# A state-space convolution and a gated MLP on one core: each queue's order written down instead of list scheduled

## The chip, the cores and the metric

The kernel runs on one core of one Trainium2 chip, in one launch. The metric is the device time in microseconds (us) from one execution; a kernel's time is the median of its runs. The core has five engines with a queue of instructions each: TensorE (PE, matmuls), VectorE (DVE), ScalarE (ACT), GpSimd (POOL) and SyncE (SP, which here only issues DMAs). ACT and POOL issue some DMAs too.

## What is computed

The reference adds three terms for x of 2048 positions and 640 channels. With `xn` the layer norm of x over the channels:

```
out = x + S4(xn) + gMLP(xn)
S4:   K[d,l] = Re( sum_n C[d,n] * exp(dt[d]*A[d,n]*l) * dt[d]*B[d,n] )     128 complex states per channel
      y = causal convolution of xn with K along the 2048 positions (by FFT of length 4096) + xn*Dskip
gMLP: z = gelu(xn @ w_in), w_in 640 x 1728;  z1, z2 = halves of z, 864 columns each
      g = w_sp @ layernorm(z2) + b_sp, w_sp 2048 x 2048
      (z1*g) @ w_out, w_out 864 x 640
```

Inputs and output are bf16.

## The kernel before, in words

**Stages.** The gMLP is made of large matmuls on the whole 128x128 array: mm1b and mm1a (xn by the two halves of w_in, 16 blocks each of 2x5 matmuls of 432 columns, followed by a gelu on ACT), ln2 (layer norm of z2 on DVE, its last step "flexible", see below), mm2 (16 blocks x 2 halves x 16 matmuls of 432 columns with w_sp, whose transposed tiles come by DMA, then one `gate` operation on DVE and a store of the gated rows to DRAM, `zg_scratch`), and mm3 (by w_out, with the gated rows read back by transposing DMAs, `zgt`).

The S4 part first generates the kernel K in two halves of ten chunks (class Kgen, `chunks` at L1234): for each chunk `trig` (sines, with small matmuls "kpe" on 32-row tiles of the array, 32x384, 32x128 and 32x272), `mags` (exponentials), `products` ("kprod", L1204, DVE), and `contract` ("kcon", L1218): 64 matmuls of 128x33 on four tiles of 32 columns, then the evacuation "kevac". The convolution is a two-stage transform (class Conv): `expand` (L1308) sends a half of K through DRAM (`k2d_scratch`) and into a layout for the transform, sixteen DMAs by SP and eight by ACT's queue, `stage1` ("st1", 128x256 on the whole array, evacuation "ev1"), `stage2` ("st2", L1352, 64x160 on two tiles of 64 rows, evacuations "ev2u" for the input and "ev2k" for the kernel, then the product "pw" on DVE), a swap of halves by DMA ("uswap"), `inverse1` ("inv1", 128x128, evacuation "evz") and the last transform "inv2" (32x160 on sixteen tiles of 32x32). inv2 and mm3 add into the same PSUM banks, and the output leaves from there.

A tile of the array is a rectangle of it with weights of its own, named by `tile_position`. In kcon and stage 2 the innermost loop runs over the tiles:

```
L1225  for jl in range(NJ):                      # 8
           for m in range(2):
               for g in range(4):
                   B.mm(pt[32*g : 32*g+NT, ...], ..., start=(m == 0), stop=(m == 1), tile_position=(0, 32*g))
L1359  for k in range(nf):
           for c in range(2):
               for jj in range(2):
                   h = 64*jj
                   B.mm(..., start=(c == 0), stop=(c == 1), tile_position=(h, 0))
```

**What sets the order.** A Builder first records every operation in program order, with what it reads and writes (5325 operations, 4282 on PE). `schedule()` (L384) then picks an order for each of the five queues, and `emit()` (L528) derives the semaphores and writes the instructions[...]. Some evacuations, copies and scalings are flexible (`flex`, L299, `flexn`, L308): they may run on ACT or on DVE, in the two engines' own instruction.

`schedule()` is a list scheduler. It keeps modelled times of each queue and each operation, and at each step picks a ready operation by priority: the longest path to the end, plus a bonus, plus an amount per kind of operation (`local`, L1734), plus an amount per group of operations (`SHIFT`, L771, 661 numbers). A change of the array's shape costs 0.095 us in its model (0.2 us when leaving 32-column tiles), a change of ACT's table 1.4 us. Flexible operations go to whichever engine is picked first, with `flexpen` (L1733) against DVE for two kinds.

The lines of the profile that follow: L341 is every matmul (`mm`), L348 PE transposes, L263 every ACT activation, L273 and L285 DVE tensor operations (L285 the gate), L293 and L304 copies, the latter flexible ones on DVE, L375 DMAs, L382 transposing DMAs. So groups are told apart by operand shape.

Of the kernel before, what the change touches and what calls it, by code (L numbers as in the profile page):

```python
# [65 lines left out]
class Builder:  # L66
# [317 lines left out]
    def schedule(self):  # L384
        ops = self.ops
        n = len(ops)
        succ = [[] for _ in range(n)]
        npred = [0] * n
        for op in ops:
            seen = set()  # L390
            for d in op.deps + op.odeps:
                if d.gidx in seen:
                    continue
                seen.add(d.gidx)
                succ[d.gidx].append(op)
                npred[op.gidx] += 1
        group = -1
        last = None
        shift = []
        for op in ops:  # L400
            if op.tag != last:
                group += 1
                last = op.tag
            shift.append(SHIFT[group] if SHIFT else 0)
        plen = [0.0] * n
        for op in reversed(ops):
            best = 0.0
            bmax = op.bonus
            for s_ in succ[op.gidx]:
                if plen[s_.gidx] > best:  # L410
                    best = plen[s_.gidx]
                if s_.bonus > bmax:
                    bmax = s_.bonus
            plen[op.gidx] = best + op.dur + (op.lat if op.is_dma else 0.0)
            op.bonus = bmax
            op.prio = plen[op.gidx] + bmax + self.local.get(op.tag, 0.0) + shift[op.gidx]
        ready = {q: [] for q in QUEUES}

        def make_ready(op):
            for q in (("act", "dve") if op.alt else (op.q,)):  # L420
                ready[q].append(op)

        for op in ops:
            op.t0 = None
            if npred[op.gidx] == 0:
                make_ready(op)
        tfree = {q: 0.7 for q in QUEUES}
        flight = {q: [] for q in QUEUES}
        CAP = 120
        cur_tab = None  # L430
        cur_mode = None
        dma_free = 0.0
        TABSW = 1.4
        MODESW = {(128, 32): 0.2}
        WIN = 2.0
        WINP = 0.1
        order = []
        petimes = []
        nsched = 0
        while nsched < n:  # L440
            bestq = None
            for q in QUEUES:
                cand = ready[q]
                if not cand:
                    continue
                evals = []
                base = tfree[q]
                if q == "pe" and len(petimes) >= 128:
                    base = max(base, petimes[-128] + 3.2)
                for op in cand:  # L450
                    ts = base + (MODESW.get(cur_mode, 0.095) if q == "pe" and op.mode != cur_mode else 0.0)
                    for d in op.deps:
                        t = d.t1 + (0.057 if q == "pe" else 0.035)
                        if t > ts:
                            ts = t
                    for d in op.odeps:
                        if d.t0 > ts:
                            ts = d.t0
                    if q == "dve" and op.alt:
                        ts += self.flexpen.get(op.tag, 0.0)  # L460
                    rt = ts
                    if q == "act" and op.tab is not None and op.tab != cur_tab:
                        ts += TABSW
                    evals.append((ts, op, rt))
                tmin = min(e[0] for e in evals)
                pick = None
                for ts, op, rt in evals:
                    if ts <= tmin + (WINP if q == "pe" else WIN):
                        if pick is None or op.prio > pick[1].prio:
                            pick = (ts, op, rt)  # L470
                gap = None
                for ts, op, rt in evals:
                    back = MODESW.get(op.mode, 0.095) if q == "pe" and op.mode != pick[1].mode else 0.0
                    if ts + op.dur + back <= pick[2 if q in ("act", "pe") else 0] + 0.02 and (gap is None or op.prio > gap[1].prio):
                        gap = (ts, op, rt)
                if gap is not None:
                    pick = gap
                if bestq is None or pick[0] < bestq[0]:
                    bestq = (pick[0], pick[1], q)
            ts, op, q = bestq  # L480
            if op.alt:
                op.q = q
                op.emit, op.dur = op.alt[q]
                if q == "dve":
                    ts -= self.flexpen.get(op.tag, 0.0)
            if q == "act" and not op.is_dma and cur_tab is None and op.tab is None:
                ts += 1.3
                cur_tab = "none"
            op.t0 = ts
            if op.is_dma:  # L490
                start = max(ts + op.dur + 0.7, dma_free)
                dma_free = start + op.lat
                op.t1 = max(dma_free, ts + op.dur + 1.0) + 1.0 + op.late
            else:
                op.t1 = ts + op.dur + (op.lat if q == "pe" else 0.083)
            tfree[q] = ts + op.dur
            if op.is_dma:
                fl = flight[q]
                fl.append((dma_free - op.lat, dma_free, op.npk))
                left = 0  # L500
                for a, b, k in reversed(fl):
                    if left + k > CAP:
                        tfree[q] = max(tfree[q], b - (CAP - left) / k * (b - a))
                        break
                    left += k
            if q == "act" and op.tab is not None:
                cur_tab = op.tab
            if q == "pe":
                cur_mode = op.mode
                petimes.append(op.t0)  # L510
            for q2 in (("act", "dve") if op.alt else (q,)):
                ready[q2].remove(op)
            order.append(op)
            nsched += 1
            for s_ in succ[op.gidx]:
                npred[s_.gidx] -= 1
                if npred[s_.gidx] == 0:
                    make_ready(s_)
        order.sort(key=lambda o: (o.t0, o.gidx))
        self.ops = order  # L520
        self.qops = {q: [] for q in QUEUES}
        for i, op in enumerate(order):
            op.gidx = i
            op.idx = len(self.qops[op.q])
            self.qops[op.q].append(op)
        self.est_time = max(o.t1 for o in order)
# [189 lines left out]
class Psum:  # L716
# [54 lines left out]
SHIFT = [  # L771
    292.2, 1391.7, 2926.2, 561.5, 4282.2, 0.0, 2464.1, 366.2, -1.3, 2095.2, 394.9, -6.4, 721.6, 288.5, 0.0, 561.5, 201.7, 7.0,
    615.9, -45.8, -1168.9, 949.4, -194.4, -36.5, -1185.4, -303.8, -215.4, 59.3, 0.0, 0.0, 2191.5, 632.2, 688.9, 1082.1, -171.1,
    -193.0, -30.1, 199.4, -1314.7, -1347.1, -3793.2, -1646.2, -27.5, -2166.0, -310.6, -2172.9, -1840.9, -5938.5, -1378.4,
    -1199.0, 680.3, 175.2, -29.4, 7463.7, 1298.2, 98.9, 91.3, 1676.7, 846.7, 1227.3, 236.0, 1866.9, -339.0, 3716.3, 147.3,
    854.7, 390.5, 2928.5, 21.9, 1945.2, 579.7, 7007.6, -488.7, -1849.5, 4059.8, 0.7, 423.9, 31.0, 2.6, -0.2, 3991.7, -466.5,
    3680.8, -1812.8, 2137.0, -1632.9, 222.4, 0.5, -1194.4, -761.7, -3318.7, -2388.7, -1746.3, -101.5, 364.7, 676.6, -60.0,
    608.1, -2172.5, -60.0, -96.1, 445.2, 2190.8, 1135.2, 583.4, 80.5, 1311.8, -117.4, -290.7, -33.9, 703.7, 415.2, 67.6, -766.3,
    -129.8, -7054.1, 229.2, -3288.8, -898.9, -330.0, -341.9, -1257.9, 105.6, -2259.6, -1176.8, 3406.7, -594.9, 843.2, -139.9,
    957.2, 2718.9, -374.2, -35.1, -885.8, 1787.8, -183.1, 3595.1, 2420.5, -292.2, -1089.0, -395.3, -1298.2, -280.3, -28.1, 21.7,  # L780
    -791.4, 0.0, 1963.3, 946.1, 1151.7, 2527.5, -408.6, -146.3, 0.0, 816.6, -66.0, 0.2, 2123.5, 0.0, -4548.3, -299.3, 772.2,
    0.0, 24.8, 25.3, -1418.1, -681.6, -1782.0, -1405.0, -49.2, -1346.2, 111.2, -649.5, 1185.3, -797.1, -524.2, -4443.6, -770.4,
    -1733.8, -2177.1, -1539.6, -435.2, -543.3, 0.0, -1346.0, 440.6, -2121.5, -700.2, 716.5, 0.0, 496.3, 772.4, -124.3, 970.3,
# [35 lines left out]
EXP_ = 2500.0  # L819
# [966 lines left out]
```

## Time and profile before

| what | value |
|---|---|
| runs of the kernel | 338.49, 340.62 and 589.61 us, median 340.62 |
| span of the profiled execution, first to last instruction | 337.6 us |
| PE busy | 314.9 us (93%), 4282 matmuls |
| PE loading weights | 210.1 us (62%) |
| DVE busy | 264.4 us (78%), 501 instructions |
| ACT busy | 230.4 us (68%), 267 instructions, 17 table loads of 1.283 us among them |
| DMA | 48.67 MB, mean 144 GB/s; 82153 of 102356 packets under 512 B |
| changes of the array's shape between matmuls in program order | 172 |
| operations that set PE's bound: 128x432 matmuls | 172.3 us for 832 |

The profiled execution's own device time is not listed apart from its span; the median of the runs is 3.0 us above this span. A row of the profile's groups names a line, an engine, an operation and the operand shapes, then count, busy time and the mean time in flight of one; several matmuls are in flight at once, so the mean is not what one costs. The end of a matmul is modelled in the trace, its start is recorded, so matmuls are best compared by the distance of their starts. "Idle before" is how long an engine stood still ahead of a group, with what released it. In the row of slices, each digit is the busy share of 1/40 of the span in tenths, and PEclk is the granted clock of PE in tenths of full speed.

### The profile page before, as it was taken

The numbers are of one execution on the slowest core, as the hardware profiler recorded it, in microseconds if no ns is written. First come the engines' busy times: TensorE is split into PE (matmuls) and PEld (weight loads), VectorE is DVE, ScalarE is ACT, GpSimd is POOL, SyncE is SP. The second block draws the span as 40 slices with busy tenths as digits, with TensorE's granted clock in tenths as the row PEclk, the third lists the DMA queues.
The fourth block names the chain that finished last, engine by engine and source line by source line (L and its number), as shares of the span: only waits on it lengthen the run. The fifth ranks groups of instructions, "written<-read, shape, count | busy, mean of one in ns | idle before, by whom it ended". The sixth has DMA issues, their size and how long they took to land.

```text
span 337.6 us, 9918 instructions
## 1 busy us (share of the span) xinstructions
PE 314.9 (93%) x4282; PEld 210.1 (62%) x4282; DVE 264.4 (78%) x501; ACT 230.4 (68%) x267; POOL 17.7 (5%) x34
## 2 busy tenths in 40 slices
PE   3999999989999999999999999997999989999972
PEld 2445467756556665556656586764689776679751
DVE  5998999998898997579999875968773676872373
ACT  3598989998665559684489976615688866337531
POOL 4211000212100000000000000000002000000001
PEclk9999999999999999999999999998999999999995
DMA  7994648544992555698899959799456999200056
GB/s 216 362 377 170 95 103 229 118 121 112 163 145 61 106 95 113 137 231 139 67 143 154 244 100 224 163 211 113 73 109 143 131 180 198 98 2 2 2 143 174
DMA packets 102356, 48.67 MB, mean 144 GB/s; under 512 B 82153, under 2 KB 100170, under 8 KB 101802
## 3 DMA queue, kind: packets, MB, share of 16 engines
q1 hardware_dynamic: 97256, 44.74, 65.6%
q0 software_dynamic: 448, 2.79, 4.7%
q10 hardware_dynamic: 4610, 0.53, 2.0%
q8 instruction: 33, 0.54, 0.7%
q14 instruction: 9, 0.07, 0.1%
HBM read 18.47 MB, written 11.61 MB: 89 GB/s over the span
## 4 chain that ended last, share of the span: by engine, by line
PE 71%; ACT 9%; DVE 7%; DMA 5%; issue 2%; ACTq 2%; SPq 2%; POOL 1%; POOLq 0%; DVEq 0%
PE ps L341 71%; ACT arena L263 6%; DVE arena L1516 3%; ACT L263 3%; DMA arena<-in_A_u_dram 3%; ACTq L375 2%; DVE arena L273 2%; SPq L382 1%; DMA arena<-xn_scratch 1%; DMA xn_scratch<-arena 1%; DVE arena L280 1%; SPq L375 1%; POOL arena L271 0%; DVE arena L285 0%; DVE arena L313 0%
## 5 line engine op out<-in xcount | busy, mean ns | idle before, releaser
L341 PE MATMUL ps<-arena 128*24 128x33 bf16 (+10 forms) x4222 | 311.8, 268 | 14.7 <-ACT arena L263 5.5
L341 PEld LDWEIGHTS ps<-arena 128*128 128x128 bf16 (+5 forms) x4222 | 206.2, 115 | 116.4 <-ACT arena L263 22.5
L263 ACT ACTIVATE arena<-ps 128x1088 bf16<-128x1088 int16 (+8 forms) x181 | 170.8, 975 | 89.5 <-PE ps L341 68.2
L273 DVE TENSOR_TENSOR arena<-arena 128x512 bf16<-128x512 bf16 (+14 forms) x199 | 121.5, 646 | 10.2 <-ACT arena L263 6.8
L304 DVE CAST arena<-ps 128x1024 bf16<-128x1024 f32 (+3 forms) x32 | 35.5, 1116 | 20.3 <-PE ps L341 19.8
L263 ACT ACTIVATE arena<-arena 128x320 bf16<-128x320 f32 (+8 forms) x69 | 39.6, 626 | 10.6 <-issue 10.0
L273 DVE TENSOR_TENSOR arena<-ps,arena 128x320 bf16<-128x320 f32 (+3 forms) x42 | 22.7, 562 | 17.6 <-PE ps L341 17.1
L1516 DVE BATCH_NORM_STATS2 arena<-arena 128x6 f32<-128x320 bf16 (+1 forms) x64 | 30.2, 538 | 3.1 <-DMA arena<-in_A_u_dram 2.9
L285 DVE SCALAR_TENSOR_TENSOR arena<-ps,arena 128x432 bf16<-128x432 f32 x32 | 21.2, 666 | 14.1 <-PE ps L341 13.9
L263 ACT ACT_TABLE_LOAD x17 | 21.8, 1283 | 2.0 <-issue 1.8
L280 DVE TENSOR_SCALAR arena<-arena 128x544 bf16<-128x544 bf16 (+5 forms) x43 | 13.2, 318 | 1.1
L375 POOL DMA_DIRECT2D arena<-in_A_u_dram x8 | 4.1, 514 | 174.5 <-PE ps L341 174.5
L271 POOL TENSOR_TENSOR arena<-arena 128x4 f32<-128x4 f32 (+2 forms) x10 | 9.6, 958 | 67.4 <-DVE arena L280 67.4
L348 PE MATMUL ps<-arena 128*128 128x128 bf16 x60 | 6.1, 238 | 2.3 <-DVE arena L280 1.9
L348 PEld LDWEIGHTS ps<-arena 128*128 128x128 bf16 x60 | 4.5, 107 | 5.1 <-DVE arena L280 2.3
L313 DVE TENSOR_SCALAR arena<-arena 128x864 bf16<-128x864 bf16 (+1 forms) x15 | 6.4, 476 | 0.1
L285 DVE SCALAR_TENSOR_TENSOR arena<-arena 128x4 f32<-128x4 f32 (+4 forms) x14 | 4.6, 330 | 1.0 <-POOL arena L271 0.9
L375 POOL DMA_DIRECT2D out_dram<-arena x2 | 1.0, 501 | 74.5 <-DVE arena L273 74.5
L304 DVE COPY arena<-arena 32x640 bf16<-32x640 bf16 (+4 forms) x13 | 4.2, 368 | 0.1
L1518 DVE BATCH_NORM_AGGREGATE arena<-arena 128x2 f32<-128x12 f32 x32 | 4.2, 176 | 0.1
L1097 DVE RECIPROCAL arena<-arena 128x640 f32<-128x640 f32 x1 | 4.2, 4153 | 0.0
L304 DVE CAST arena<-arena 128x640 bf16<-128x640 f32 (+1 forms) x5 | 3.0, 622 | 0.0
(10 smaller groups left out, 6.0 us busy)
## 6 DMA issues: line engine op xcount, KB each, us to landing
arena<-arena SPq DMA_DIRECT2D x12, 360.0 KB, 6.5
zg_scratch<-arena SPq DMA_DIRECT2D x16, 216.0 KB, 3.0
xn_scratch<-arena SPq DMA_DIRECT2D x4, 640.0 KB, 5.9
arena<-in_A_u_dram POOLq DMA_DIRECT2D x8, 320.0 KB, 8.0
arena<-xn_scratch SPq DMA_DIRECT2D x8, 320.0 KB, 7.2
arena<-in_A_u_dram SPq DMA_DIRECT2D x3, 640.0 KB
out_dram<-arena SPq DMA_DIRECT2D x16, 120.0 KB, 3.4
arena<-c_c SPq DMA_DIRECT2D x1, 1536.0 KB, 10.1
```

Of the source, the lines that this page charges most:

```text
L263: return e.activation(out, in_, func, bias=bias, scale=scale)
L271: return self._add(q, lambda e: e.tensor_tensor(out, in0, in1, op), [in0, in1], [out], dur=d, port=True)
L273: return self._add(q, lambda e: e.tensor_tensor(out, in0, in1, op), [in0, in1], [out], dur=self._dve_cost("tt", out, [in0, in1]), port=port)
L280: return self._add(q, lambda e: e.tensor_scalar(out, in0, s1, s2, op0, op1), self._aps(in0, s1, s2), [out], dur=self._dve_cost("ts", out, ...
L285: return self._add("dve", lambda e: e.scalar_tensor_tensor(out, in0, scalar, in1, op0, op1), self._aps(in0, scalar, in1), [out], dur=self. ...
L304: "dve": (lambda e: e.tensor_copy(out, in_), self._dve_cost("ts", out, [in_]))}
L313: "dve": (lambda e: e.tensor_scalar(out, in_, scale, bias, ALU.mult, ALU.add), self._dve_cost("ts", out, [in_]) + 0.11)}
L341: op = self._add("pe", lambda e: e.matmul(out, lhsT, rhs, start=start, stop=stop, **kw), [lhsT, rhs], [out], dur=d)
L348: op = self._add("pe", lambda e: e.transpose(out, in_, ident), [in_, ident], [out], dur=0.09, lat=0.3)
L375: op = self._add(q, lambda e: e.dma_start(out, in_), [in_] + list(wait), [out], is_dma=True, dur=0.66 if self.tag == "expand" else 0.57, l ...
L1097: B.generic("dve", lambda e: e.reciprocal(t3, pp), [pp], [t3], dur=4.2)
L1516: B.generic("dve", (lambda e, c=c: e.bn_stats(st[:, a, c, :], src[:, a, w * c:w * c + w])), [src[:, a, w * c:w * c + w]], [st[:, a, c, :]] ...
```

## The change

`schedule()` no longer chooses. A table `ORDER` lists for each queue the numbers of its operations, as runs "first:count" in the order of their recording, and so also says which engine each flexible operation runs on. What is left of the loop walks the five lists with a simple time model only to find one overall sequence of emission in which each operation comes after those it depends on. `SHIFT`, `local` and `flexpen` go. `emit()`, which sets the semaphores, is unchanged, and so are all the functions that record operations.

```diff
     def schedule(self):
         ops = self.ops
-        n = len(ops)
-        succ = [[] for _ in range(n)]
...
-            op.prio = plen[op.gidx] + bmax + self.local.get(op.tag, 0.0) + shift[op.gidx]
-        ready = {q: [] for q in QUEUES}
...
-        TABSW = 1.4
-        MODESW = {(128, 32): 0.2}
...
+        left = {}
+        for q in QUEUES:
+            left[q] = []
+            for run in ORDER[q].split():
+                a, _, n = run.partition(":")
+                left[q] += ops[int(a):int(a) + int(n or 1)]
+            for op in left[q]:
+                if op.alt:
+                    op.q = q
+                    op.emit, op.dur = op.alt[q]
+                op.t0 = None
+            left[q].reverse()
...
+        while len(order) < len(ops):
+            best = None
+            for q in QUEUES:
+                op = left[q][-1] if left[q] else None
+                if op is None or any(d.t0 is None for d in op.deps + op.odeps):
                     continue
+                ts = max([tfree[q]] + [d.t1 + 0.05 for d in op.deps] + [d.t0 for d in op.odeps])
...
+                if best is None or ts < best[0]:
+                    best = (ts, q)
+            ts, q = best
+            op = left[q].pop()
...
-SHIFT = [
-    292.2, 1391.7, 2926.2, 561.5, 4282.2, 0.0, 2464.1, 366.2, -1.3, 2095.2, 394.9, -6.4, 721.6, 288.5, 0.0, 561.5, 201.7, 7.0,
...
+ORDER = {
+    "pe": """
+        205:10 195:10 193 192 38:5 348:10 51:5 69:8 78:2 364:3 359:2 367:2 361:3 370:2 375:5 372:3 381:10 101:2 110:2 103:6
...
-    B.flexpen = dict(eva=1.0, kevac=0.5)
-    B.local = dict(ln1=5000.0, xnt=3000.0, prepa=5500.0, exps=EXP_, prep=1500.0, mm1b=2000.0, gelu2=4500.0, gelu1=3200.0, kcon=1000.0, kevac=1000.0, kpe=1500.0, gate=1000.0, load=2000.0, ln2=800.0, prepf=4700.0, load0=6000.0, expand=3000.0)
     B.emit()
```

What the two compiled programs show side by side:

- Changes of the array's shape: 172 before, 141 after. Stretches of tiled matmuls between full-array ones: 78 before, 60 after. Of them on 64-row tiles 29 and 19; kcon runs 20 (64 matmuls each) and 18 (20 to 108 matmuls each); on 32x32 tiles 4 and 3. After, 22 changes lead from 32-row tiles straight to 32-column tiles or back.
- The order inside tiled runs. Consecutive matmuls on the same tile: kcon 0 and 622, stage 2 4 and 290, inv2 1 and 193, kpe 80 and 24. An example out of ORDER is kcon chunk 0, `829 833 837 841 ...` and then `826 830 834 838 ...`: sixteen matmuls of one column group, then sixteen of another.
- The engine of flexible operations: 69 change it, so that ACT has 254 instead of 271 operations and DVE 518 instead of 501.
- On ACT, the eight DMAs of the second `expand` stand in one block ahead of the first ev2k evacuations before; after, four of them do, and the others come between later operations. Between the two gelus around 69 us stand eight exponentials before and five after.
- On SP, the transposing loads `zgt` of the gated rows come later in the queue; the seven of the last quarter of the positions stand behind that quarter's gate and four other DMAs.
- Layer-norm blocks 12 to 15 of the input come before blocks 8 to 11.

## The prediction

> **What bounds the kernel now.** I read the page's busy table and its 40 slices first, to see which engine fills the span, and then the chain of waits.
>
> ```profile
> PE 314.9 (93%) x4282; PEld 210.1 (62%) x4282; DVE 264.4 (78%) x501; ACT 230.4 (68%) x267; POOL 17.7 (5%) x34
> ...
> PE   3999999989999999999999999997999989999972
> ...
> PEclk9999999999999999999999999998999999999995
> ...
> PE 71%; ACT 9%; DVE 7%; DMA 5%; issue 2%; ACTq 2%; SPq 2%; POOL 1%; POOLq 0%; DVEq 0%
> ```
>
> TensorE is busy in 93% of the span, has one slice below 8 outside the two ends, and carries 71% of the chain. The time is TensorE's work plus its few gaps, so I count three things: matmul time, time lost when the array changes shape, and gaps. Matmul time by operand shape comes from the groups, shapes kept apart (PE rows; columns: count, busy us, mean ns, idle before):
>
> ```profile
> L341 PE MATMUL ps<-arena 128*128 128x432 bf16 x832 | 172.3, 353 | 3.6 <-ACT arena L263 2.0 <-DMA arena<-in_B_w_in_dram 0.7 <-DMA arena<-xn_scratch 0.4
> ...
> L341 PE MATMUL ps<-arena 128*24 128x33 bf16 x1280 | 25.0, 234 | 0.0
> L341 PE MATMUL ps<-arena 64*128 64x160 bf16 x512 | 23.8, 235 | 2.4 <-ACT arena L263 2.4
> ...
> L341 PE MATMUL ps<-arena 32*32 32x160 bf16 x512 | 9.5, 252 | 3.4 <-issue 1.9 <-ACT arena L263 1.1 <-DVE arena L273 0.2
> ```
>
> The mean is the time one matmul is in flight; what it costs is busy time by count. 128x33 (kcon, 32-column tiles) costs 25.0/1280 = 20 ns though each is in flight 234 ns, so several tiles work at once. The largest gap is read from the timeline:
>
> ```profile
> 222.71 7.59 ACTq L375 DMA_DIRECT2D arena<-k2d_scratch  x8
> ...
> 230.40 0.73 ACT L263 ACTIVATE arena<-arena 64x640 bf16<-64x640 bf16 x1 [9.96 <-issue]
> 231.14 2.78 ACT L263 ACTIVATE arena<-ps 128x960 bf16<-128x960 f32 x3
> ...
> 232.17 4.56 PE L341 MATMUL ps<-arena 64*128 64x160 bf16 x53 [2.39 <-ACT arena L263]
> ```
>
> ACT's queue spends 7.59 us issuing eight DMAs; the activation behind them, then the evacuation of PSUM that stage 2 needs, start late, and PE stands still for 2.39 us. Stretches of time (length; busy and count of PE, PEld, DVE, ACT, POOL; granted clock; DMA share; GB/s) give the prices:
>
> ```profile
> 90.16:91.27 1.11, 1.11 (x65) 1.05 (x65) 1.08 (x3) 0.42 (x1) 0.00 (x0) 1.00 1.40 289
> 101.84:103.34 1.50, 1.50 (x65) 1.44 (x65) 1.43 (x4) 0.41 (x1) 0.00 (x0) 1.00 0.84 115
> ...
> 229.40:233.00 3.60, 1.21 (x27) 0.81 (x24) 1.99 (x2) 2.59 (x4) 0.00 (x0) 1.00 1.54 96
> 233.00:236.00 3.00, 3.00 (x27) 1.39 (x23) 3.00 (x4) 1.89 (x2) 0.00 (x0) 0.51 1.21 144
> 82.50:123.40 40.90, 40.79 (x711) 24.23 (x711) 36.92 (x72) 24.65 (x26) 2.13 (x4) 1.00 0.72 113
> 123.40:146.00 22.60, 22.46 (x329) 13.20 (x328) 14.88 (x32) 18.59 (x30) 0.00 (x0) 1.00 0.59 132
> ```
>
> A kcon run of 64 takes 1.11 us, a few take 1.50; in those, 22 matmuls start 34 ns apart instead of 15[...]. After the gap, PE runs 3 us at clock 0.51. In kernel generation, 82.5 to 123.4, DVE is busy 36.9 of 40.9 us, close behind PE.
>
> [...] full-array matmuls of 432 columns start 183 ns apart, the first tiled one after them 93 to 96 ns later than that, and the start after a tiled run comes 150 to 254 ns after the run's last one, by shape. [...] a kpe run (32-row tiles) has 384, 64x2 columns per row group in program order, yet at 86.812 four 384-column matmuls of four row groups start within 20 ns and the four 128-column ones 173 ns later. Matmuls of one tile pass waiting ones of another, up to six of them here. [...] here a gap of about 2.5 us was enough, and the 432-column matmuls then took 360 ns instead of 183. [...]
>
> **The change part by part.** No operation is added or removed; four things move.
>
> *Shape changes.* Side by side, excursions from the full array fall from 78 to 60: 64-row ones 29 to 19, kcon runs 20 to 18, 32x32 ones 4 to 3; 22 changes now lead from 32-row straight to 32-column or back. Entries 18 × 0.095 = −1.7. Exits: stage 2 runs of 12 and 36 take 521 and 1352 ns, so 34.7 ns a matmul and 105 ns fixed (the exit), 10 × 0.105 = −1.05; kcon 2 × 0.15 = −0.3; 32x32 1 × 0.17. Sum −3.2. It comes off PE's path wherever PE is busy without a break, which is nearly everywhere.
>
> *Order inside runs.* Before, kcon cycles the four column groups and stage 2 alternates the two row halves: consecutive matmuls on the same tile number 0 and 4. Afterwards they number 622 in kcon (sixteen on one column group, then sixteen on the next), 290 in stage 2 (six to twelve on one half) and 193 in inv2, while kpe falls from 80 to 24. If PE picks matmuls past blocked ones, it costs nothing. If it doesn't, kcon falls from 15 to at best the 34 ns pace, 622 × 19 = +11.8, and stage 2 from 34.7 to the 67 ns of one half alone (twice the alternating pace), 290 × 32 = +9.3: +21. Bounds 0 and +21, plus up to +8.5 for inv2 (193 × 44 ns), which I leave out of the middle[...]. I take 0: passing was seen six deep, though not sixteen, and not within column groups. Kcon runs also get longer, up to 108: [...] I take +2.5 (0 to +5).
>
> *ACT's DMAs.* Only four of the eight issues stand ahead of the evacuations, so the block is about 3.8 us instead of 7.6. The wait of 2.46 us (start to start) goes, and with it the half clock: 3 us at 0.51 lost about 1.5. Together −4.0 (0 if the wait only moves: the other four issues stand ahead of later evacuations, which then are late next). Ahead of the gelu at 69 us stand five exponentials instead of eight, 1.1 us less ACT work, against a PE wait of 1.34: −0.7 (−1.3 to 0). The wait of 1.08 at 272, stage 1 on an evacuation by ACT, −0.5 (−1.1 to 0), since 17 evacuations net move from ACT to DVE.
>
> *DVE and transfers.* DVE gets some 5.4 us more before the last kernel products (6.3 in, 0.9 out). Its cover is its idle time, 4.0 of 40.9 us and 7.7 of 22.6 in the two stretches; it fits, but not where kernel products come one after another: +1 (0 to +5). The transposing loads of the last quarter of zg move on SP behind its gate and four more DMAs; seven issues at 1.28 us and a latency of 3 to 10 us land 19 to 26 us after the gate, and PE has 23.9 us of other work: +1 (0 to +3). Layer-norm blocks 12 to 15 now come before 8 to 11, which makes the last spill some 3 us earlier and the activations of blocks 8 to 11 1 to 2 us later; together with the start: +1 (−1 to +2). The weight, u, expansion and swap transfers are issued with room before their users: 0, hidden by full-array matmuls; without that cover one is worth 3 to 8 us, its landing time. The table loads stay 17, at 1283 ns each.
>
> Sum: −3.2 + 0 + 2.5 − 4.0 − 0.7 − 0.5 + 1 + 1 + 1 = −2.9. From the span of 337.6 to 334.7; the median of the runs, 340.62, lies 3.0 above that span, and I keep this distance: 337.7 us.
>
> **Rivals.** (1) *PE serialises matmuls of one tile* (slower). +21 on top of −2.9 is 358.7, say 358; +2% of 340.6 is 6.8, so it decides once 9.7 of the 21, 46%, come true. For it: sixteen in a row is deeper than anything in this trace, no 32-column run in it has two in a row[...]. Against it: the kpe run and, at 232.17, stage 2 matmuls of one half that started ahead of the other. (2) *New waits*: DVE becomes the bound in kernel generation at +5 rather than +1, zg at +3 rather than +1: 337.7 + 6 = 343.7, less if one comes alone: 343. For it: 36.9 of 40.9 busy. Against: PE work of other kinds is interleaved there. (3) *Better*: no fill cost (−2.5), zg and DVE fully hidden (−2), start gained (−2): 331. For it: nothing in those terms is a measured wait. Against: all must hold.
>
> **How the numbers follow.** Chances: forecast 0.45, rival 1 0.36, rival 2 0.12, rival 3 0.07. The likeliest gives 337.7, its own range 332 to 344. The whole range, 332 to 358, leaves out about half of rival 1's upper side (0.15) and half of rival 3 (0.05). Two per cent, about what a measurement here can tell from no change, puts the bounds at 333.8 and 347.4. Faster: 0.07 of rival 3 and 0.06 of the forecast, 0.13. Slower: nearly all of rival 1 (0.34), 0.04 of rival 2 and forecast: 0.38. Same: 0.49.
>
> **What would show it.** In the groups, 128x33 near 27 us and 64x160 near 22.7 if tiles overlap; near 37 and 33 if not (then rival 1, and the total with it). Shape changes: the span falls where 64-row excursions vanished. The ACT step: no PE wait above 1 us on ACT before stage 2 of the second half, and no PEclk dip in mid-span; a wait of similar size later means it moved. Rival 2: PE idle before kcon, released by DVE L273. A PE wait on a DMA out of zg_scratch at the first mm3 refutes that step. What would make the forecast wrong most is any tiled run paced by one tile.

## The result, and the profile after

The changed kernel takes 360.2 us (median of 5 runs, 359.02 to 365.23), the kernel before 340.62; the ratio is 1.062, 95% interval 1.054 to 1.070. It is slower by 6%. (Some executions of one and the same kernel are slower than the rest; ratios and intervals here leave them out, so a ratio isn't exactly the quotient of two medians.) The forecast was 337.7 us, the range 332 to 358: wrong, and just outside the range. The first rival, that PE serialises matmuls of one tile, had 358.

The page of the changed kernel: busy table, two rows of slices, and the chain by engine.

```profile
PE 340.7 (94%) x4282; PEld 242.2 (67%) x4282; DVE 275.8 (76%) x518; ACT 214.3 (59%) x250; POOL 17.7 (5%) x34
...
PE   2989999899999999999999999999989979999993
...
PEclk9999999999899998989999899999999989999995
...
PE 83%; SPq 7%; ACT 4%; DMA 3%; DVE 2%; issue 1%; POOL 0%; POOLq 0%; DVEq 0%
```

Between the two profiled executions the span grew by 23.2 us (337.6 to 360.8; the medians of the runs lie 19.6 apart), and PE's busy time by 25.8 (314.9 to 340.7), with the same matmuls. PE doesn't wait longer; the same work takes longer. And PEclk, 9 in all of the first 27 slices before, now has an 8 in the 11th, 16th, 18th and 23rd (the one in the 33rd follows a wait in mm3). The groups say which matmuls it is:

```profile
L341 PE MATMUL ps<-arena 128*128 128x432 bf16 x832 | 170.2, 357 | 2.2 <-ACT arena L263 2.1
L341 PE MATMUL ps<-arena 128*24 128x33 bf16 x1280 | 46.9, 233 | 0.1
L341 PE MATMUL ps<-arena 128*128 128x320 bf16 x224 | 36.4, 305 | 3.8 <-DMA arena<-zg_scratch 3.8
L341 PE MATMUL ps<-arena 64*128 64x160 bf16 x512 | 25.7, 234 | 0.0
```

The 128x33 matmuls (kcon) went from 25.0 to 46.9 us; their mean time in flight is 233 ns as before. One matmul takes as long as it did, but fewer are in flight at once. Stage 2 (64x160) rose only from 23.8 to 25.7 and lost its 2.4 us wait on ACT, and mm3 (128x320) now waits 3.8 us on the gated rows from DRAM.

Summing the distance from each matmul's start to the next one's, by kind (called "from start to start" below), gives the whole difference of the spans: kcon +21.7, mm3 +2.8, stage 2 +2.6, xn transposes +1.6, mm1a +1.1, mm1b −3.4, mm2 −1.4, stage 1 −1.2, kpe −0.9, the rest +0.3; together +23.2.

Stretches of the changed kernel (columns as in the prediction): one kcon run and what follows it, a kcon run in the recorded order, and two stage 2 runs of 36.

```profile
92.75:97.41 4.66, 4.66 (x102) 4.56 (x99) 3.16 (x8) 1.08 (x1) 0.00 (x0) 1.00 0.72 179
97.41:101.00 3.59, 3.59 (x23) 1.44 (x21) 2.04 (x4) 1.45 (x1) 0.00 (x0) 0.53 0.53 111
109.06:110.57 1.51, 1.51 (x78) 1.41 (x74) 0.84 (x2) 1.31 (x1) 0.00 (x0) 1.00 0.00 0
248.77:250.69 1.92, 1.92 (x38) 1.79 (x37) 1.69 (x2) 0.06 (x1) 0.00 (x0) 1.00 1.22 198
252.82:254.33 1.51, 1.51 (x38) 1.38 (x37) 1.33 (x2) 0.60 (x1) 0.00 (x0) 1.00 1.25 106
```

The first run has 96 kcon matmuls, sixteen at a time on one column group: 4.66 us. The third stretch has 73 of them, 64 cycling the groups: 1.51 us. In the first run, the starts of the records lie 58 ns apart on one group (0, 70, 127, 190, ... 599, 657, 715 ns); the first start that belongs to the next group comes at 721, right behind the thirteenth, when only three of the sixteen are still waiting. After that run the clock is 0.53 for some 3.5 us, though PE had been busy without a break. The two stage 2 runs differ by how long they stay on one half: two blocks of six and two of twelve cost 1.92 us, six blocks of six 1.51, and the kernel before had 1.35 for alternating ones.

### The profile page after: what moved, and what is told of

The parts are those of the page before. It is cut to its first block, busy times and chain, and to the rows that moved or that the text cites. A ratio compares the mean times of both kernels' runs of the same rounds, so it can differ in the third digit from the quotient of the medians.

```text
span 360.8 us, 9933 instructions
## 1 busy us (share of the span) xinstructions
PE 340.7 (94%) x4282; PEld 242.2 (67%) x4282; DVE 275.8 (76%) x518; ACT 214.3 (59%) x250; POOL 17.7 (5%) x34
## 4 chain that ended last, share of the span: by engine, by line
PE 83%; SPq 7%; ACT 4%; DMA 3%; DVE 2%; issue 1%; POOL 0%; POOLq 0%; DVEq 0%
PE ps L341 82%; SPq L382 6%; ACT arena L263 3%; DMA arena<-in_A_u_dram 1%; DMA arena<-zg_scratch 1%; PE ps L348 1%; DVE arena L273 1%; SPq L375 1%; ACT L263 1%; DVE arena L1519 0%; DVE arena L285 0%; POOL out_dram L375 0%; POOLq L583 0%; DVE arena L280 0%; DVE arena L304 0%
## 5 line engine op out<-in xcount | busy, mean ns | idle before, releaser
L341 PE MATMUL ps<-arena 128*24 128x33 bf16 (+9 forms) x4222 | 336.6, 269 | 12.5 <-DMA arena<-in_A_A_re_dram 4.7
L341 PEld LDWEIGHTS ps<-arena 128*128 128x128 bf16 (+4 forms) x4222 | 237.8, 115 | 108.9 <-issue 27.0
L263 ACT ACTIVATE arena<-ps 128x1024 bf16<-128x1024 f32 (+7 forms) x171 | 161.5, 980 | 137.6 <-PE ps L341 131.8
L273 DVE TENSOR_TENSOR arena<-arena 128x192 bf16<-128x192 bf16 (+14 forms) x199 | 122.6, 646 | 22.0 <-ACT arena L263 10.8
L304 DVE CAST arena<-ps 128x1024 bf16<-128x1024 f32 (+3 forms) x42 | 44.5, 1066 | 27.6 <-PE ps L341 24.9
L1519 DVE BATCH_NORM_STATS2 arena<-arena 128x6 f32<-128x320 bf16 (+1 forms) x64 | 31.0, 533 | 3.9 <-DMA arena<-in_A_u_dram 3.9
L263 ACT ACTIVATE arena<-arena 128x320 bf16<-128x320 f32 (+12 forms) x62 | 32.1, 575 | 0.8 <-DVE arena L285 0.3
L263 ACT ACT_TABLE_LOAD x17 | 21.8, 1283 | 2.5 <-issue 2.2
L313 DVE TENSOR_SCALAR arena<-arena 128x864 bf16<-128x864 bf16 (+1 forms) x21 | 9.0, 485 | 0.2
L304 DVE COPY arena<-arena 32x960 bf16<-32x960 bf16 (+4 forms) x16 | 5.8, 374 | 0.3
L297 POOL MEMSET arena<- 128x320 bf16 (+3 forms) x9 | 2.8, 344 | 0.3 <-POOLq L1772 0.3
```

The costliest lines, as they stand in the source:

```text
L263: return e.activation(out, in_, func, bias=bias, scale=scale)
L273: return self._add(q, lambda e: e.tensor_tensor(out, in0, in1, op), [in0, in1], [out], dur=self._dve_cost("tt", out, [in0, in1]), port=port)
L304: "dve": (lambda e: e.tensor_copy(out, in_), self._dve_cost("ts", out, [in_]))}
L313: "dve": (lambda e: e.tensor_scalar(out, in_, scale, bias, ALU.mult, ALU.add), self._dve_cost("ts", out, [in_]) + 0.11)}
L341: op = self._add("pe", lambda e: e.matmul(out, lhsT, rhs, start=start, stop=stop, **kw), [lhsT, rhs], [out], dur=d)
L1519: B.generic("dve", (lambda e, c=c: e.bn_stats(st[:, a, c, :], src[:, a, w * c:w * c + w])), [src[:, a, w * c:w * c + w]], [st[:, a, c, :]] ...
```

## Experiments

All are tables of order for the same operations; the computation is unchanged in every one of them. Theory A, from the starts just shown: a matmul waits for the one before it on its tile, and PE looks past only a few waiting ones. Theory B: kcon is slow because its runs became longer (64 matmuls each before, up to 108 after).

### The kcon order put back

```diff
 pe:  ... 891 893 892 894
-     829 833 837 841 845 849 ... 889 826 830 834 ... 886 827 831 ... 887 920 924 ...
+     826:64 918:32
      896:12 1883:9 ...
```

> The changed kernel with only the kcon matmuls put back into recorded order, so that they cycle the four column groups; they stand in the same 1280 places of PE's list. Theory A (a matmul on a tile waits for the one before it on that tile, and PE looks past only a few waiting ones): kcon falls from 45.6 us to about 25, the half-clock stretches after long kcon runs (about 4.4 us lost) go, time about 360.2 - 21 - 4 = 335. Theory B (kcon is slow because its runs are longer[...]): kcon stays near 45, time about 360.

Measured: 339.8 us, ratio to the kernel before 1.002 (0.999 to 1.006). Of the 6.2% excess, 6.0 are gone. Groups and clock row of this kernel:

```profile
PEclk9999999999999999999999999999979999999996
...
L341 PE MATMUL ps<-arena 128*24 128x33 bf16 x1280 | 30.2, 230 | 0.2
```

Theory A holds, B falls as the main cause: the runs have the same lengths as in the changed kernel. The 8s of the clock row in the first 23 slices are gone too (the 7 in the 30th follows a wait of 2.5 us in mm3); in the changed kernel, four of the six kcon runs of 3.5 us or more were followed by a stretch at about half clock, in which the 432-column matmuls lost some 4.4 us in all against their usual 183 ns from start to start. But kcon is still 5.1 us above the kernel before (29.0 against 23.9 from start to start), and the time is 340, not 335.

### Stage 2 alternating again, alone and with kcon

```diff
-     3617 3619 3621 3623 3625 3627 3616 3618 3620 3622 3624 3626 3603 3605 ...
+     3588:12 3602:12 3616:12
```

> The changed kernel with only the stage 2 matmuls sorted within each run, so that the two row halves alternate again. Theory A: stage 2 falls from 24.4 us to 512 x 34.7 ns + 19 exits x 0.105 us, about 20 us, time about 356. Theory B: no change, 360.

Measured: 360.0 us, ratio 1.062 (1.056 to 1.068), the same as the changed kernel.

```profile
L341 PE MATMUL ps<-arena 128*128 128x320 bf16 x224 | 35.6, 300 | 5.3 <-DMA arena<-zg_scratch 5.3
L341 PE MATMUL ps<-arena 64*128 64x160 bf16 x512 | 22.2, 230 | 0.6 <-ACT arena L263 0.5
```

Stage 2 fell by 3.0 us from start to start (24.4 to 21.5), and the span of the profiled execution by 2.8, but the four runs show no gain; by their interval they can't tell one of up to some 3 us from none. In this trace, mm3 waits 5.3 us for the gated rows instead of 3.8: half of what PE saves ahead of these loads it waits at them.

> Both of the edits in the changed kernel. Theory A: 335 - 4 = 331, that is below the kernel before by some 9 us, since 31 changes of shape and the wait on ACT before stage 2 are gone while zg waits of about 4 us remain. If the other steps of the change were worth nothing: 340. Theory B: 360.

Measured: 338.1 us, ratio 1.001 (0.997 to 1.005). With all tiled runs but inv2 cycled, the changed order is neither better nor worse than the kernel before. So the rest of the change is worth about nothing, where I had forecast −2.9.

### How many waiting matmuls PE looks past

The kernel before, with the kcon runs in blocks of g on one column group, for example at g = 4:

```diff
-     826:64
+     826 830 834 838 827 831 835 839 828 832 836 840 829 833 837 841:2 846 ...
```

> The order of the kernel before, written down, but within each of its 20 kcon runs of 64 each column group gets blocks of g matmuls in a row, g = 4,5,6,8,16,2,3,4,5,6,8,16,2,3,4,5,6,8,16,1 in order of time, and the seven stage 2 runs of 36 have blocks g = 4,5,6,3,1,2,6 on each row half. Theory A1 (each tile has room for three waiting matmuls[...]): a kcon run takes about 1.1 us for g up to 4, 1.2 at 5, 1.5 at 6, 2.2 at 8, 3.15 at 16; stage 2 1.35 us up to 4, 1.41 at 5, 1.48 at 6; the whole about 340.6 + 11.5 = 352. Theory A2 (PE looks past at most three waiting matmuls in all): 1.25 us at 4, 1.7 at 5 and 6, 2.2 at 8, 3.1 at 16. Theory B (length of the run): all kcon runs 1.1 to 1.5 us, time 340.6.

Stretches of this kernel: kcon runs of 64 at g = 4, 5, 6, 8 and 16, and what follows another run at 16.

```profile
129.61:130.71 1.10, 1.10 (x65) 1.00 (x65) 1.05 (x4) 0.42 (x1) 0.00 (x0) 1.00 0.53 119
138.31:139.64 1.33, 1.33 (x65) 1.23 (x65) 1.25 (x5) 1.32 (x2) 0.00 (x0) 1.00 0.50 113
144.21:145.83 1.62, 1.62 (x66) 1.52 (x65) 0.00 (x0) 0.23 (x1) 0.00 (x0) 1.00 0.44 87
160.14:162.49 2.35, 2.35 (x65) 2.25 (x65) 2.07 (x4) 1.33 (x1) 0.00 (x0) 1.00 0.52 115
163.69:166.91 3.22, 3.22 (x65) 3.12 (x65) 1.51 (x3) 0.79 (x1) 0.00 (x0) 1.00 0.70 123
...
206.45:209.00 2.55, 2.55 (x75) 2.06 (x73) 1.81 (x2) 1.34 (x2) 0.00 (x0) 0.61 0.04 7
```

| g | 1 | 2 | 3 | 4 | 5 | 6 | 8 | 16 |
|---|---|---|---|---|---|---|---|---|
| us of a run of 64 | 1.12 | 1.18, 1.19 | 1.09, 1.21 | 1.10, 1.12, 1.33 | 1.32, 1.32, 1.33 | 1.62, 1.62, 1.69 | 2.32, 2.35, 2.37 | 3.20, 3.20, 3.22 |
| A1, estimate with three waiting per tile | 1.1 | 1.1 | 1.1 | 1.1 | 1.2 | 1.5 | 2.2 | 3.15 |
| A2, estimate with three in all | – | – | – | 1.25 | 1.7 | 1.7 | 2.2 | 3.1 |

A2 was worked out from g = 4 on. At 5 the two theories are 0.5 us apart and A1 is nearer by far; two of three runs at 4 are at A1's value too, and the measured runs lie 0.05 to 0.19 us above A1 at 5 to 16. The three is an estimate of mine. It can be told from its neighbours with this case's own figures (58 ns from start to start on one column group in the changed kernel; in the kernel before, 15.5 ns from start to start with the groups cycled and 150 ns from the last start to the next full-array one): two per tile give 1.9 us at 5 and 2.7 at 8, three 1.3 and 2.3, four 1.3 and 1.9; measured are 1.32 to 1.33 and 2.32 to 2.37. Stage 2 runs of 36 took 1.36 at g = 3, 1.37 at 4, 1.44 at 5, and 1.64 and 1.67 at 6 (1.46 and 1.45 in the same places in the kernel before). The time was 348.5 us in the one run, against 352 expected; kcon took 34.9 us from start to start, 11.0 more than in the kernel before, against 11.5 expected. Run lengths are unchanged here, so length has no part in it. Two of the three runs at 16 (3.2 us each) were followed by half clock, one at 0.61 in the last line, and none of those at 8.

Why some of the serial runs are followed by half clock and others not was not shown. The trace of the changed kernel has half clock five times in mid-span, 3.41 us each, from 97.41, 138.37, 155.43, 199.81 and 291.97 on; the last follows the wait of 2.35 us in mm3, the other four a serial kcon run that had filled the 3.41 us ahead, or 2.9 of them at 199.81. But the run of 87 at 115.90, 4.23 us long at 47 ns a matmul, has full clock behind it, and so has the run of 107 at 202.76, 3.54 us at 32 ns. And the run of 96 that half clock follows in the changed kernel is as slow in the kernel with stage 2 alternating (4.64 us against 4.66), and there nothing follows:

```profile
92.38:97.02 4.64, 4.64 (x100) 4.54 (x97) 3.16 (x8) 1.08 (x1) 0.00 (x0) 1.00 1.44 157
97.02:100.60 3.58, 3.58 (x50) 2.50 (x49) 2.40 (x4) 1.45 (x1) 0.00 (x0) 1.00 0.74 111
```

### Where the rest of the gain went: the gated rows

```diff
 sp:  ... 2229
-     4311 1773 3552:4 4307 1775 2264 4317 ... 2315 4308 ... 2420 4325 4319 4322:2 4329 4326 4332 4330 4328 4327 4331
+     4305 1773 3552:4 4306 1775 2264 4307 ... 2315 4319 ... 2420 4322:11
```

> The kernel with kcon and stage 2 cycled (e3_both_cycled), and on SP the 28 transposing loads of the gated rows in the order in which mm3 needs them, first quarter first, in the same 28 places of SP's list. If PE's waits on zg_scratch (2.5 and 0.7 us in e3_both_cycled, start to start) are on the path: they go, 338.1 - 3 = 335. If they are hidden by the tail or come back as a wait on another load: 338.

Measured: 340.3 us, ratio 1.007 (1.004 to 1.011): not faster, but 0.4 to 1.1% slower than the kernel before. Waits of PE in the kernel with both edits, in this one, and in the next one (us in total, times, longest):

```profile
PE ps L341 <- DMA arena<-zg_scratch: 2.9, 2, 2.3
```

```profile
PE ps L341 <- DMA arena<-zg_scratch: 3.5, 3, 2.1
```

```profile
PE ps L341 <- DMA arena<-zg_scratch: 3.2, 3, 2.3
```

In the kernel with both edits, SP issues the first quarter's last load only at 243.4, behind loads and stores of later quarters and 0.6 us after mm3 has begun, and PE waits for it. In order, that wait is gone, but eleven loads now stand behind the last gate, and PE waits for the last three.

> The kernel with kcon and stage 2 cycled (e3_both_cycled), and the last 59 DMAs of SP before the second swap (the transposing loads of the gated rows, their stores, the expansion and the swaps) in the sequence of the kernel before, so that only seven loads stand behind the last gate, and not eleven as in e5_zg_loads_in_order. If SP's late issues are what makes mm3 wait: no wait on zg_scratch above 0.5 us, 338 - 3 = 335. If the loads are late for another reason, such as the landing times themselves: waits of 2 to 4 us stay, 338 to 340.

Measured: 341.8 us, ratio 1.013 (1.007 to 1.018): slower than the kernel before by about 1%. The waits stayed, for the last three loads of the last quarter. SP issued the store behind the last gate 8.5 us after that gate (249.0 to 257.5) and the first load 8.2 us later, where the kernel before took 3.6 and 2.4; PE needs the rows 22 to 24 us after the gate in both. So the order on SP alone doesn't cure it. By the trace, SP spends 7.3 of the 8.5 us on issuing five other loads, and 7.4 of the 8.2 us waiting for a store of gated rows to land, where the kernel before waits 1.7. Why that landing took so much longer stays open.

### The length of kcon runs

```diff
-     826:64 918:32 896:12 1883:9 950:32 ...
+     826:64 896:12 1883:9 918:64 ...
```

> e3_both_cycled with three long kcon runs cut: the sizes 96,32 and 73,87,32 and 99,29 become 64,64 and 64,64,64 and 64,64; the rest of the order is the same. If the length of a run makes its last matmuls come at 34 ns instead of 15: kcon falls from 29.1 to about 26.3 us, the time by 2.8 to 335. If the 34 ns pace has another cause (what ran before the run): kcon stays at 28 to 29 us, 338.

Measured: 337.4 us, ratio 0.998 (0.995 to 1.001). Kcon took 28.4 us from start to start: 0.7 less, where 2.8 were expected of the length. The run of 108 in this kernel takes 1.76 us, 16 ns a matmul, while seven runs of 64 take about 1.5 us with 21 to 25 matmuls 34 ns apart. A long run with the fast pace and short ones with the slow pace stood in the first experiment too; here 96 and 108 matmuls:

```profile
92.19:94.78 2.59, 2.59 (x100) 2.53 (x96) 2.59 (x6) 1.08 (x1) 0.00 (x0) 1.00 1.37 217
138.98:140.75 1.77, 1.77 (x114) 1.71 (x111) 0.86 (x2) 1.56 (x2) 0.00 (x0) 1.00 0.05 10
```

The same runs have the same pace in every trace of this order, so something about the place in the order decides it, and not the length alone. What about the place does, I could not find: neither the matmuls ahead of a run nor how long its data had been ready sorts the slow from the fast. It stays open, at 5 us of the span.

> Both edits of the two kernels ahead of it. If both are on the path: 338.1 - 3 - 2.8 = 332; if neither is: 338.

Measured: 340.7 us, ratio 1.006 (1.002 to 1.009). It adds nothing to either.

### The wait before stage 2 in the kernel before

```diff
 act: ... 3550
-     3568:8 3581 3600 3614 3670 3656 3712 3642 3698 ...
+     3568 3570 3572 3574 3581 3600 3614 3670 3656 3573 3712 3642 3571 3575 3698 ... 3787 3569 ...
```

> The order of the kernel before, written down, with one edit: of the eight expansion DMAs on ACT, four (every second one) stand later, between the evacuations, where the changed kernel has them. If the block of eight made PE wait 2.46 us and lose 1.5 us more at half clock: both go, 339.1 - 4 = 335. If the wait only moves to a later evacuation or to the later loads: 339, and a wait of similar size stands elsewhere before stage 1 of the kernel's second half.

Measured: 336.3 us, ratio 0.997 (0.995 to 1.000).

> The order of the kernel before, written down as a table and with nothing else changed: its instructions are those of the kernel before. It shows what the edits made on this base are measured from, and whether the wait of 2.46 us before stage 2 and the half clock after it stand in a second profile too. If writing the order down has no cost: 338 to 339, ratio 1.000. If the gap and the half clock belong to every execution: both are there again.

Measured: 337.5 us, ratio 1.002 (0.998 to 1.006), so writing the order down costs nothing that shows. Timelines, first of the order before in its second profile, then of the one with fewer DMAs on ACT:

```profile
223.16 6.68 ACTq L375 DMA_DIRECT2D arena<-k2d_scratch  x8
...
231.71 2.49 PE L341 MATMUL ps<-arena 64*128 64x160 bf16 x41 [1.48 <-ACT arena L263]
```

```profile
223.59 3.29 ACTq L375 DMA_DIRECT2D arena<-k2d_scratch  x4
226.99 0.73 ACT L263 ACTIVATE arena<-arena 64x640 bf16<-64x640 bf16 x1 [5.66 <-PE ps L341]
```

In the second profile of the same order the block took 6.68 us instead of 7.59, PE waited 1.48 instead of 2.39, and the stretch after it is at full clock:

```profile
233.00:236.00 3.00, 3.00 (x39) 1.67 (x34) 3.00 (x4) 2.41 (x3) 0.00 (x0) 1.00 1.23 141
```

With four DMAs ahead, PE doesn't wait there. The mechanism is as forecast; its worth is the difference of the two ratios, 0.4%, about 1.5 us. By the two intervals it lies between 0 and 3 us, so it can't be told from nothing, and is below the 4 of the forecast. None of the orders tried here beats the kernel before by more than its interval; this edit comes nearest.

## Why the prediction was wrong, point by point

**The step that failed** is *Order inside runs*, and in it the sentence "I take 0: passing was seen six deep". The reading of the kpe run was wrong. Its list is 384 and 128 columns for the first row group, the same for the second, the third and the fourth. Six matmuls do stand ahead of the fourth group's first, but three of them were running; it passed three waiting ones, one on each of three row groups. I read the six as a depth for the queue as a whole. The times of the experiment on g are nearest to the estimate with three waiting matmuls on each tile (1.32 us at five in a row, 2.35 at eight). And sixteen in a row on one column group are serial for the first thirteen: they start 58 ns apart, and the next group's first only at 721 ns. That costs 16.6 us in kcon (45.6 against 29.0 from start to start), where I had put 0. In inv2, which I had left out, the 193 cost nothing that shows (12.3 and 12.4 us from start to start).

**Rival 1** had the right cause and nearly the right time, but by errors that cancel. I priced a blocked kcon matmul at 34 ns, the pace of the slow stretches; it is the 58 ns at which one tile starts matmuls of 33 columns, so kcon lost 16.6 instead of 11.8. Stage 2 was priced at 9.3 and lost 3.0 at most from start to start, since blocks of six still overlap in part (1.51 us for 36; at 69 ns from start to start, the pace on one half alone at 249.3 to 249.7 in the changed kernel, they would take about 2.5), and in one trace half of it came back as mm3's waits. And the half clock after long serial runs, 4.4 us, was in no case. Ahead of that half clock PE's record shows no idle time at all, 4.66 us of 4.66 busy, and the clock still fell to 0.53 in the 3.59 us behind. So a busy digit in the profile is no cover. What the four stretches ahead of half clock have in common is a kcon run at 38 to 49 ns a matmul (in the kernel before, cycled ones go at 14 to 22); that this alone isn't enough is shown by the run at 115.90, at 47 ns.

**Fill of long runs**, their late matmuls at 34 ns (+2.5, 0 to +5, an estimate of mine): +5.1, so just beyond the end, and not because of their length alone (a run of 108 goes at 16 ns a matmul, runs of 64 have the slow pace too). The cause is open.

**ACT's DMAs** (−4.0): the wait is gone, as forecast, but mis-sized: it was 1.5 us in a second profile of the same order and had no half clock behind it; the runs give about 1.5, between 0 and 3. I took one execution's gap and its clock for a constant. That gap, 229.78 to 232.17, lay wholly in the 3.41 us ahead of its half clock, which starts at 233.06. The gelu at 69 us (−0.7) gave nothing: PE waits 1.45 us there (lost against the usual distance), before 1.34. The wait at 272 (−0.5) is gone, but a second profile of the order before doesn't have it either.

**Transfers** (+1, up to +3): 4.2 us of lost starts in mm3 in the changed kernel, beyond the end, and with the wrong load named: the first long wait is for the first quarter's last load, behind loads and stores of later quarters, and the longest (2.5 us) for one of the third quarter; the last quarter, which I had worked out, takes 0.5.

**DVE** (+1): no PE wait on DVE stands ahead of kcon in the changed kernel; nothing. **The start** (+1): mm1b −3.4, against xn transposes +1.6, mm1a +1.1, the first matmul 0.9 later and other preparation +0.2; +0.4.

**Shape changes** (−3.2): not isolated. kpe, whose runs now lead straight into kcon, is 1.9 us cheaper with both edits; stage 2, with ten excursions fewer, is not (21.8 against 21.9), since its runs there lose to waits inside and to 24 pairs that are still not alternating. That the kernel with both edits is level with the one before (1.001) says only that the sum of all these terms is about zero.

**The base** was about 1 us too high: I added the 3.0 us between one execution's span and the median of others. In the five runs of the changed kernel, the time of an execution lies 1.8 to 2.6 us above its own span.

What the chances said: 0.36 for this rival. The case against it rested mostly on one pattern, and the pattern had an explanation that limited it: in that kpe run, each tile that was passed had one waiting matmul, not several.

## What to carry to other kernels

In the tiled runs of this kernel, order was throughput: 64 kcon matmuls took 1.12 us cycled and 3.20 to 3.22 with sixteen in a row on one column group. Cycle the tiles inside every run, and give no tile more than four matmuls in a row (the most that cost little or nothing in the two shapes tried here: 1.10, 1.12 and once 1.33 us for kcon, 1.37 for 36 of stage 2 against 1.35 in the kernel before); a planner that counts changes of shape and not tiles can trade a few microseconds, 3.2 by the forecast here, for twenty (360.2 us against 339.8 with kcon cycled). When one trace shows an engine passing something blocked, ask how many were waiting on each of its lanes, before using that for a longer row. Count only the waiting ones, not those that had started. And take a gap or a stretch at half clock from two profiles before it goes into a sum as a constant.

## What the runs showed of the hardware that I had not expected

- Runs of 64 matmuls on four column groups take 1.10 to 1.33 us with four in a row on one group, 1.3 with five, 1.6 to 1.7 with six, 2.3 to 2.4 with eight and 3.2 with sixteen. With sixteen in the changed kernel, the next group's first start comes behind the thirteenth, 721 ns into the run.
- One column group starts a 33-column matmul every 58 ns (changed kernel, run at 92.75); four of them together one every 15 (kernel before, 64 in 1.11 us).
- Half clock followed stretches in which PE was busy without a break, but mostly on one column group at a time: four of six of 3.5 to 4.7 us in the changed kernel, two of three of 3.2 us with blocks of sixteen, none of 2.3 to 2.4 with blocks of eight. In the changed kernel each stretch of half clock in mid-span lasted 3.41 us.
- Two profiles of the same order differ by 3.5 us in span (337.6 and 334.1).
